# P V of the W2 lanes moved behind them, with ten lent buffers

## The chip, the core and the metric

The kernel runs on one NeuronCore of one Trainium2 chip. The metric is the device time of one execution in microseconds (us). A profile of one execution stands beside the times: it shows each engine's instructions (PE = TensorE matmul, PEld = its weight loads, DVE = VectorE, ACT = ScalarE, POOL = GpSimd, SP = SyncE, which here only issues DMAs), and L12 means line 12 of the kernel.

## What is computed

A transformer block on x of 2048 rows and 576 columns, bf16, with 32 heads of 18 columns, a sliding window of 256 keys, and a gated MLP of width 4608:

```python
def _A_ref(x, wqkv, wo):
    B, S, D = x.shape
    H = 32; Dh = D // H; W = 256
    qkv = (lambda x, *d: x.transpose(*d))((x @ wqkv).reshape(B, S, 3, H, Dh), 2, 0, 3, 1, 4)
    q, k, v = qkv[0], qkv[1], qkv[2]
    scores = jnp.einsum("bhqd,bhkd->bhqk", q, k) * (Dh ** -0.5)
    idx = jnp.arange(S)
    mask = (idx[:, None] - idx[None, :] >= 0) & (idx[:, None] - idx[None, :] < W)
    scores = jnp.where(mask[None, None], scores, -1e9)
    p = _softmax(scores, axis=-1)
    o = jnp.einsum("bhqk,bhkd->bhqd", p, v)
    return (lambda x, *d: x.transpose(*d))(o, 0, 2, 1, 3).reshape(B, S, D) @ wo

def _B_ref(x, w1, w3, w2):
    gate = jnp.einsum("bsd,df->bsf", x, w1)
    up = jnp.einsum("bsd,df->bsf", x, w3)
    h = _silu(gate) * up
    return jnp.einsum("bsf,fd->bsd", h, w2)

x = A_x
xn = _layernorm(x, axis=-1)
return x + _A_ref(xn, A_wqkv, A_wo) + _B_ref(xn, B_w1, B_w3, B_w2)
```

## The kernel before

The rows are worked in four chunks of 512 (c = 0 to 3). The 32 heads are eight groups of four (g = 0 to 7), and two groups make a pair j. Every operation is recorded with `add` (engine, keys read, written and joined), and `resolve` turns the keys into semaphore waits; each engine runs its own operations in the recorded order, SP's DMA queue too. Buffers of the same kind are told apart by keys such as `("w13", 1)`, and a writer waits for the last readers of its key.

A chunk goes through these stages:

- **Gate/up**, 36 units (`unit_pairs`, L860; `unit_tanh`, L869; `unit_h`, L875 and L878). A unit is 9 pairs of 64-row matmuls into one of three pairs of PSUM banks, which `job()` hands out in turn; unit u + 3 takes unit u's banks. The weights come in sets of 512 columns, four units each, in three buffers `w13`; `load_part` (L343) issues the next part, and from chunk 1 on a set has two parts of 576 KB. Between the pairs stand score steps of groups 4 to 7 (`scores` L682, `exps` L691, `masks` L718), and late in the stage their P V (`pv`, L739), two pairs in a row.
- **Projections** of the next chunk's q, k and v (`proj_part`, L496). `pair_of` says which two of nine column tiles one q projection makes; `new_k` and `new_q` copy keys and queries of groups 0 to 3 from `stage` to their places by DMA.
- **W2 lanes** (`w2_lanes`). The array works as four row tiles of 32 rows, one lane each, with W2 (L1036) and the output projection (L1045) in four passes d_ of 128 output columns. A planner with a clock for each lane writes the order: it takes the lane that is least far, and puts in score steps of the next chunk's groups 0 to 3 (`score_new` L756, `exps_new` L763 on ACT, `masks_new` L771 on DVE), 48 of them, at least `W2_SPACE` apart. Two steps share a buffer from `slots`, 14 of them. One round of the lanes is a matmul in each; after round numbers in `events` come repacks of the keys of groups 4 to 7 (`span_main` L585, `span_last` L616; nine, from round 40, 12 apart), the sums of a finished pass sent by a DMA transpose (`turn`, L1119), and at rounds 148 and 156 the two parts of the next chunk's second weight set. `finish` sums a pass's four banks on ACT and DVE (L987 to L992).
- When 24 steps are done and `PV_WAIT` is over, **P V of groups 0 and 1** (`pv_new(n, 0, ...)`, L791, 48 matmuls over all 128 rows and 32-column tiles) stands among the lanes. All lanes stop for it. Its output is emptied by `pv_out` (a transpose on DVE, L800), divided in `o_scale` (L805 on DVE, L806 on POOL) and turned back in `o_turn` (L813); its 12 slots are then used again.
- The **rest of W2**, its last 64 columns (`b = sets[0][0]`, 41 steps of two column tiles, L1086 and L1096), then **P V of groups 2 and 3** (L791), and `orem`/`frem` take the 64 columns out (L1105, L1106).

The next chunk's gate/up then starts with what is left over: x of the old chunk is loaded (`load_four`, L315), the late P V is emptied, and work is put behind unit u by `later(u, ...)`: turns in units 0 and 1, `o_pack` and `o_rest` (L817, DMAs on SP) in units 1 to 5, and the sum with x (`fin_add`, L1130 and L1132; `fin_store`, L1137) in units 4 to 7. Layernorm statistics of the chunk after (`ln_stats`, L391 to L394) start in unit 8 of chunks 1 and 2. The last chunk has no lanes and ends with a stage of its own.

Of the kernel before, what the change touches and what calls it, by code (L numbers as in the profile page):

```python
# [5 lines left out]
dt = mybir.dt  # L6
# [4 lines left out]
_DEBUG = {}  # L11
# [153 lines left out]
def bass_parallel_sum__sliding_block__glu_gated_swiglu__prompt_kernel(  # L165
# [32 lines left out]
    with ExitStack() as es:  # L198
# [39 lines left out]
        def pt_slot(sl):  # L238
            kind, n = sl
            if kind == "pt":  # L240
                return pt[:, n, :, :]
            if kind == "w2":
                return w2[n][:, :, :].rearrange("p f d -> p (f d)")[:, 0:2 * CH].rearrange("p (q r) -> p q r", r=2)
            if kind == "xs":
                return xpb[:, n:n + 2, :].rearrange("p t d -> p (t d)")[:, 0:2 * CH].rearrange("p (q r) -> p q r", r=2)
            if kind == "od":
                return od[n][:, :, :].rearrange("p g c -> p (g c)").rearrange("p (q r) -> p q r", r=2)
            if kind == "sh":
                two = stage[:, 2 * n:2 * n + 2, :]
            else:  # L250
                two = hT[:, NF - 8 + 2 * n:NF - 6 + 2 * n, :]
            return two.rearrange("p t c -> p (t c)").rearrange("p (q r) -> p q r", r=2)

        def pt_keys(sl):
            kind, n = sl
            if kind in ("pt", "w2", "od"):
                return [(kind, n)]
            if kind == "xs":
# [209 lines left out]
        def pair_of(c, i):  # L468

            return (((0, 1), (2, 3), (8, 4), (5, 6)) if c == 0 else ((8, 0), (1, 2), (3, 4), (5, 6)))[i]  # L470

# [486 lines left out]
        def w2_lanes(c, live, pool_):  # L958
# [17 lines left out]
            rounds = 0  # L976
            pv_done = False
# [20 lines left out]
            while any(at[a] < len(items[a]) for a in range(4)):  # L998
# [57 lines left out]
                if a == 3:  # L1056
                    rounds += 1
                    for what in events.pop(rounds, ()):
                        w2_side(c, what)
                if not pv_done and 0 in ended and not any(tail) and min(at) > 2 * 41 + 5 and now > ended[0] + PV_WAIT:  # L1060
                    pv_done = True
                    _DEBUG.setdefault("st", []).append((c, "pv", round(max(clk), 2), d_, at[:]))
                    cand = sorted(sets[1 - d_ % 2], key=lambda x: ready[x])[:2]
                    t = max(clk)
# [11 lines left out]
                    for g in (0, 1):  # L1076
                        for s in range(3):
                            slots.extend(pt_of[(n, g, s, pr)] for pr in range(2))
            assert pv_done and done == len(steps), (c, pv_done, done)
            _DEBUG.setdefault("w2", []).append((c, round(max(clk), 2), ended, [round(x - max(clk), 2) for x in clk]))  # L1080
            b = sets[0][0]
            for k in range(41):
                for r in range(2):
                    if k < NF:
                        sl = (c * 2 * NFC + 16 + k // 18) % NW2
                        add("pe", lambda e, k=k, r=r, sl=sl: e.matmul(  # L1086
                            PS[64 * r:64 * r + 64, b, 0:256], w2_by(sl, 64)[:, k % 18, :], hT[:, k, 256 * r:256 * r + 256],
                            start=(k == 0), stop=False, tile_position=(0, 64 * r), skip_group_check=True),
                            r=[("h", k), ("w2", sl)], **{"j" if k or r else "w": [("ps", b)]})
                        if r and k % 18 == 17:  # L1090
                            load_w2((c + 1) * 2 * NFC)
                    else:
# [4 lines left out]
                            PS[64 * r:64 * r + 64, b, 0:256], wt, oT[:, t, 256 * r:256 * r + 256],  # L1097
                            start=False, stop=(t == 4), tile_position=(0, 64 * r), skip_group_check=True),
# [17 lines left out]
        def w2_side(c, what):  # L1116
            if what[0] == "turn":
                d_ = what[1]
                add("sp", lambda e: e.dma_start_transpose(fin[:, :, d_ * 128:(d_ + 1) * 128], gs[d_ % 2][:]),  # L1119
                    r=[("gs", d_ % 2)], dma=f"tr{d_}", **{"j" if d_ else "w": [("fin", k) for k in range(TB)]})  # L1120
            elif what[0] == "repack":
                k = what[1]
                (span_main if k < 5 else span_last)(GN, G, only=slice(k if k < 5 else k - 5, (k if k < 5 else k - 5) + 1))
            else:
                load_part()

# [165 lines left out]
        W2_FIRST, W2_SPACE, PV_WAIT = 2.2, 0.53, 3.0  # L1292
        W2_REPACK, SEND_AFTER = 40, 15
        W2_EVENTS = {148: (("part",),), 156: (("part",),)}
        late_pv = None

        for c in range(NC):
# [23 lines left out]
            early = [("sh" if c else "h", n) for n in range(4)] + [("w2", (c * 2 * NFC + n) % NW2) for n in range(NW2)]  # L1321
            if c:
                free += [("od", n) for n in range(NOD)]
            side = {}
# [167 lines left out]
            if c + 1 < NC:  # L1492
# [12 lines left out]
                for m, what in enumerate(PROJ_LATER + [None]):  # L1505
# [82 lines left out]
```

## Time and profile before

| what | value |
|---|---|
| three runs, median (lowest to highest) | 554.21 us (553.2 to 554.61) |
| the profiled execution | 553.22 us |
| its span, first to last instruction | 551.5 us |
| lanes between chunks 1 and 2, with the P V inside | 251.3 to 290.6 us |
| 64-column rest of W2 | 290.6 to 295.2 us |
| second P V | 295.2 to 296.6 us |
| first L860 of chunk 2 | 296.6 us |
| granted clock of PE | 1.0 |

In the rows of the timeline the first number is the start, the second the duration, both in us, then engine, line, operation, what is written and read, and how many rows were merged. A matmul's end is modelled and overlaps the next one, so its pace is read from starts. In the groups by line stand the busy time in us, the mean of one in ns, and the idle time before. In the waits stand the total, the number and the longest. "SPq" and "ACTq" are DMA issues; "to landing" is the time from issue until the data have arrived.

### The profile page before, as it was taken

What the parts mean: (1) busy time and instruction counts of PE and PEld (TensorE: products, weight loads), DVE (VectorE), ACT (ScalarE), POOL (GpSimd) and SP (SyncE); (2) the same over time, 40 slices, a digit from 0 to 9 for tenths busy, and PEclk for the clock granted to TensorE, in tenths of its full rate; (3) what the DMA queues carried; (4) which work ended last, traced back from release to release, by engine and by line L of the source; (5) the groups of instructions that cost most, each with busy time, mean ns of one, the idle gap of its engine ahead of it and who ended that gap; (6) DMA issues with size and microseconds to landing.
All of it is one profiled execution on the core that took longest, in us unless ns stands there. A gap on an engine that the chain in (4) does not pass through costs nothing.

```text
span 551.5 us, 17660 instructions
## 1 busy us (share of the span) xinstructions
PE 547.4 (99%) x7690; PEld 302.4 (55%) x7690; DVE 364.5 (66%) x745; ACT 294.5 (53%) x481; POOL 120.5 (22%) x281
## 2 busy tenths in 40 slices
PE   8999999999999999999999999999999999999998
PEld 4555545465564444555556444455555644454776
DVE  6566988746748877874665887786466676688011
ACT  6457776267827565236883655533787376523000
POOL 5613644200013332110001333211000233210000
PEclk9999999999999999999999999999999999999999
DMA  9997999558699999395769999928687988845452
GB/s 232 205 209 147 201 195 187 130 111 165 130 181 196 196 182 172 73 181 119 152 136 201 195 188 183 163 57 172 139 169 140 183 178 170 165 111 137 130 151 64
DMA packets 166070, 88.12 MB, mean 160 GB/s; under 512 B 101546, under 2 KB 163754, under 8 KB 165994
## 3 DMA queue, kind: packets, MB, share of 16 engines
q1 hardware_dynamic: 164622, 85.42, 79.1%
q10 hardware_dynamic: 1372, 1.59, 1.2%
q8 instruction: 60, 0.98, 0.8%
q14 instruction: 16, 0.13, 0.1%
HBM read 71.30 MB, written 2.36 MB: 134 GB/s over the span
## 4 chain that ended last, share of the span: by engine, by line
PE 98%; DMA 1%; SPq 0%; ACT 0%; issue 0%; DVE 0%
PE ps L860 51%; PE ps L1036 17%; PE ps L496 10%; PE ps L932 6%; PE ps L682 4%; PE ps L1086 2%; PE ps L1045 2%; PE ps L739 2%; PE ps L791 2%; PE ps L756 1%; DMA wv<-in_A_wqkv_dram 1%; PE ps L939 1%; PE ps L1096 0%; SPq L311 0%; ACT xnT L447 0%; PE ps L846 0%
## 5 line engine op out<-in xcount | busy, mean ns | idle before, releaser
L860 PE MATMUL ps<-xnT,w 64*128 64x512 bf16 x1400 | 177.0, 376 | 0.0
L860 PE MATMUL ps<-xnS,w 64*128 64x512 bf16 x1120 | 147.8, 376 | 0.0
L875 DVE SCALAR_TENSOR_TENSOR gs<-thb,ps 128x512 bf16<-128x512 bf16 x144 | 97.8, 679 | 60.6 <-ACT thb L869 60.0
L869 ACT ACTIVATE thb<-ps 128x512 bf16<-128x512 f32 x144 | 85.6, 595 | 77.1 <-PE ps L860 76.2
L1036 PE MATMUL ps<-hT,w 32*128 32x512 bf16 x1728 | 106.9, 374 | 0.0
L860 PEld LDWEIGHTS ps<-xnT,w 64*128 64x128 bf16 x1400 | 67.2, 94 | 70.2
L878 DVE SCALAR_TENSOR_TENSOR hT<-gs,ps 128x512 bf16<-128x512 bf16 x144 | 98.9, 687 | 5.0
L860 PEld LDWEIGHTS ps<-xnS,w 64*128 64x128 bf16 x1120 | 53.9, 94 | 58.1
L1036 PEld LDWEIGHTS ps<-hT,w 32*128 32x128 bf16 x1728 | 57.6, 92 | 29.6 <-issue 1.4
L763 ACT ACTIVATE pt<-ps 128x512 bf16<-128x512 f32 x120 | 65.1, 594 | 7.7 <-PE ps L756 7.5
L691 ACT ACTIVATE pt<-ps 128x1024 bf16<-128x1024 f32 (+1 forms) x46 | 46.2, 1005 | 33.5 <-PE ps L682 33.4
L756 PE MATMUL ps<-qv,kn 18*128 18x384 bf16 (+2 forms) x288 | 54.5, 267 | 0.0
L806 POOL TENSOR_TENSOR oq<-uq,rden 128x288 bf16<-128x288 f32 x12 | 8.1, 678 | 194.2 <-DVE rden L805 194.2
L771 DVE TENSOR_TENSOR pt<-pt,kv 128x256 int32<-128x256 int32 x96 | 31.3, 371 | 24.5 <-ACT pt L763 24.1
L718 POOL TENSOR_TENSOR pt<-pt,mk 128x128 int32<-128x128 int32 (+1 forms) x82 | 33.2, 426 | 41.3 <-ACT pt L691 41.3
L496 PE MATMUL ps<-xnT,wp 64*128 64x512 bf16 (+1 forms) x360 | 38.2, 355 | 0.1
L932 PE MATMUL ps<-w,hT 128*128 128x288 bf16 (+1 forms) x292 | 36.9, 284 | 0.0
L756 PEld LDWEIGHTS ps<-qv,kn 18*128 18x128 bf16 x288 | 26.5, 93 | 14.4 <-DVE uq L800 0.8
L932 PEld LDWEIGHTS ps<-w,hT 128*128 128x128 bf16 x292 | 28.2, 98 | 7.4 <-issue 0.5
L682 PE MATMUL ps<-qv,kv 64*128 64x320 bf16 (+4 forms) x336 | 31.7, 258 | 0.0
L813 DVE STREAM_TRANSPOSE od<-oq 128x256 bf16<-128x256 bf16 x64 | 25.4, 425 | 5.5 <-POOL oq L806 5.5
L990 DVE TENSOR_TENSOR thb<-ps,thb 128x512 f32<-128x512 f32 x24 | 16.6, 692 | 18.4 <-ACT thb L987 17.8
(132 smaller groups left out, 529.7 us busy)
## 6 DMA issues: line engine op xcount, KB each, us to landing
w<-in_B_w_dram SPq DMA_DIRECT2D x60, 576.0 KB, 6.9
w<-in_B_w_dram SPq DMA_DIRECT2D x72, 288.0 KB, 3.9
w<-in_B_w_dram SPq DMA_DIRECT2D x12, 192.0 KB, 6.1
xp<-in_A_x_dram SPq DMA_DIRECT2D x4, 576.0 KB, 4.6
xnS<-xnT SPq DMA_DIRECT2D x8, 256.0 KB, 4.8
xp<-in_A_x_dram SPq DMA_DIRECT2D x14, 144.0 KB, 4.0
oT<-od SPq DMA_DIRECT2D x56, 36.0 KB
w<-in_B_w_dram SPq DMA_DIRECT2D x6, 320.0 KB, 5.2
```

The lines of the kernel that those rows point to most:

```text
L496: op = add("pe", lambda e, out_=out_, st=st, mv=mv, n=n, r0=r0, first=first: e.matmul(out_, st, mv, start=first, stop=(part == 1 and n == ...
L682: add("pe", lambda e, r0=r0, out_=out_, kb=kb, q0=q0, nb=nb: e.matmul(out_, kb4[r0:r0 + 64, g - GN, kb + NV - NB, :] if kb < 0 else kv[r0: ...
L691: add("act", lambda e: e.activation(pt_slot(sl)[:, 0:w, :], PS[:, SC[0]:SC[1] + 1, 0:w].rearrange("p r q -> p q r"), ACT.Exp, scale=scale) ...
L718: add("pool", lambda e, vb=vb, mm=mm: e.tensor_tensor(vb, vb, mm, ALU.mult), r=(key if n == 0 else []) + ["mk"], **{"w" if n == 0 else "j" ...
L756: add("pe", lambda e: e.matmul(PS[:, b, c0:c0 + nb * 128], kn[32 * a:32 * a + Dh, g, W + 128 * jb:W + 128 * jb + 128], qv[32 * a:32 * a + ...
L763: add("act", lambda e: e.activation(head_of(sl, p), PS[:, b, :], ACT.Exp, scale=scale), r=[("ps", b)], **{"j" if p else "w": pt_keys(sl)})
L860: op = add("pe", lambda e, n=n, r0=r0, r=r, k=k, src=src: e.matmul(PS[:, b0 + r, :], wt[r0:r0 + 64, k, fl * 128:(fl + 1) * 128], src, star ...
L869: add("act", lambda e: e.activation(th[i][:], PS[:, bg, :], ACT.Tanh, scale=0.5), r=[("ps", bg)], w=[("th", i)])
L875: add("dve", lambda e: e.scalar_tensor_tensor(out=gs[i][:], in0=th[i][:], scalar=1.0, in1=PS[:, bg, :], op0=ALU.add, op1=ALU.mult), r=[("t ...
L878: add("dve", lambda e: e.scalar_tensor_tensor(out=hT[:, u, :], in0=gs[i][:], scalar=0.5, in1=PS[:, bu, :], op0=ALU.mult, op1=ALU.mult), r= ...
L932: add("pe", lambda e: e.matmul(bank, hT[:, f, tt * 128:(tt + 1) * 128], w2[sl][:, k, n0:n1], start=first, stop=(c + 1 == NC and half == 1 ...
L1036: add("pe", lambda e, b=b, rows=rows, wt=wt, fl=fl, k=k, a=a, first=first: e.matmul(PS[:, b, :], wt[rows, fl, :], hT[rows, k, :], start=fi ...
```

## The change

P V of groups 0 and 1 is no longer among the lanes. Both P Vs stand behind the rest of W2, one behind the other, ahead of gate/up. Scoring has 24 slots: new are eight of the nine rows of `w13[1]` ("wt", four), four of the five rows of the old chunk's `xnT` ("xT", two), `od` (two), and one more each from the x and the stage tiles. The two parts of the second weight set wait for the last matmul of the rest of W2 (`load_part((end,))`). The repacks start at round 36 and stand 14 apart. In the rest of W2 the five output-projection steps stand in the middle. `pair_of` is the same for all chunks, and `new_k(0)` and `new_q` come one projection earlier. In the next chunk four banks are emptied instead of two, the turns stand in units 0 to 3, `load_four` in unit 2, `o_pack` and `o_rest` in units 2 to 6, `fin_add` in units 7 to 10, and two `pt` slots serve as `uqs` until unit 3.

```diff
+            if kind == "wt":
+                return w13[1][:, 2 * n:2 * n + 2, :].rearrange("p k f -> p (k f)").rearrange("p (q r) -> p q r", r=2)
+            if kind == "xT":
+                return xnT[:, n // 2, 2 * (n % 2):2 * (n % 2) + 2, :].rearrange("p k f -> p (k f)").rearrange("p (q r) -> p q r", r=2)
...
-            return (((0, 1), (2, 3), (8, 4), (5, 6)) if c == 0 else ((8, 0), (1, 2), (3, 4), (5, 6)))[i]
+            return ((0, 1), (2, 3), (8, 4), (5, 6))[i]
...
-            slots = [("pt", k) for k in range(NPT)] + [("xs", 0), ("xs", 3), ("sh", 0), ("sh", 1)]
+            lent = [(("wt", k), [("w13", 1)]) for k in range(4)] + [(("xT", 2 * (c % 2) + k), xk(c)) for k in range(2)]
+            for sl, keys in lent:
+                P.bufs[sl] = _Gen([], None)
+                P.bufs[sl].readers = [o for k in keys for o in P.bufs[k].writers + P.bufs[k].readers]
+            slots = [("xs", k) for k in (0, 2, 4)] + [sl for sl, _ in lent] + [("pt", k) for k in range(NPT)]
+            slots += [("od", k) for k in range(NOD)] + [("sh", k) for k in range(3)]
...
-            events = {k: list(v) for k, v in W2_EVENTS.items()}
+            events = {}
             for k in range(9):
-                events.setdefault(W2_REPACK + 12 * k, []).append(("repack", k))
+                events.setdefault(W2_REPACK + W2_STEP * k, []).append(("repack", k))
...
-                if not pv_done and 0 in ended and not any(tail) and min(at) > 2 * 41 + 5 and now > ended[0] + PV_WAIT:
-                    pv_done = True
...
-                    pv_new(n, 0, cand)
-                    clk = [t + PV_NEW] * 4
-                    for x in (0, 1):
-                        pv_out(cand[x], x)
-                        ready[cand[x]] = t + PV_NEW + (1.2, 1.9)[x]
-                    o_scale(0)
-                    o_turn(0, 0)
-                    o_turn(0, 1)
-                    o_scale(1)
-                    o_turn(1, 0)
-                    o_turn(1, 1)
...
-            for k in range(41):
+            for k in [*range(18), *range(NF, NF + 5), *range(18, NF)]:
...
-            banks = job()
-            pv_new(n, 1, banks)
+            banks = [job(), job()]
+            end = last_pe()
+            for j in range(2):
+                pv_new(n, j, banks[j])
+            for j in range(2):
+                load_part((end,))
+            for sl, keys in lent:
+                for k in keys:
+                    P.bufs[k].readers += [o for o in P.bufs[sl].readers if o not in P.bufs[k].readers]
...
-        W2_REPACK, SEND_AFTER = 40, 15
-        W2_EVENTS = {148: (("part",),), 156: (("part",),)}
+        W2_REPACK, W2_STEP, SEND_AFTER = 36, 14, 15
...
-                fin_xs[:] = load_four(c - 1)
-                pv_out(late_pv[0], 0)
-                pv_out(late_pv[1], 1)
+                for m in range(2):
+                    sl = free.pop()
+                    uqs[2 + m:] = [pt_slot(sl).rearrange("p q r -> p (q r)").bitcast(dt.float32)]
+                    uq_keys[2 + m:] = [pt_keys(sl)]
+                    later(3, lambda sl=sl: free.append(sl))
+                pv_out(late_pv[0][0], 0)
+                pv_out(late_pv[0][1], 1)
                 o_scale(0)
-                later(0, lambda: (o_turn(2, 0), o_turn(2, 1), o_scale(1)))
-                later(1, lambda: (o_turn(3, 0), o_turn(3, 1)))
-                later(1, lambda: o_pack(0, "sp"))
+                pv_out(late_pv[1][0], 2)
+                pv_out(late_pv[1][1], 3)
+                later(2, lambda c=c: fin_xs.__setitem__(slice(None), load_four(c - 1)))
+                later(0, lambda: (o_turn(0, 0), o_turn(0, 1), o_scale(1)))
+                later(1, lambda: (o_turn(1, 0), o_turn(1, 1), o_scale(2)))
+                later(2, lambda: (o_pack(0, "sp"), o_turn(2, 0), o_turn(2, 1), o_scale(3)))
+                later(3, lambda: (o_turn(3, 0), o_turn(3, 1)))
                 for n in range(7):
-                    later(2 + n // 3, lambda n=n: o_rest(n, "sp"))
-                later(5, lambda: o_pack(1, "sp"))
+                    later(3 + n // 3, lambda n=n: o_rest(n, "sp"))
+                later(6, lambda: o_pack(1, "sp"))
                 for tt in range(TB):
-                    later(4 + tt, lambda tt=tt, c=c: (fin_add(tt), fin_store(c - 1, tt - 1) if tt % 2 else None))
+                    later(7 + tt, lambda tt=tt, c=c: (fin_add(tt), fin_store(c - 1, tt - 1) if tt % 2 else None))
...
-                    if got == ("q", 2):
+                    if got == ("q", 1):
                         new_k(0)
+                    elif got == ("q", 2):
                         new_k(1)
...
-                    if 3 <= m < 7:
-                        new_q(m - 3, "act")
+                    if 2 <= m < 6:
+                        new_q(m - 2, "act")
```

More of the change, by code (lines that the diff above doesn't have):

```diff
@@ L256, in pt_keys @@
             if kind in ("pt", "w2", "od"):
+                return [(kind, n)]
+            if kind in ("wt", "xT"):
                 return [(kind, n)]
@@ L1059, in w2_lanes @@
                         w2_side(c, what)
-                if not pv_done and 0 in ended and not any(tail) and min(at) > 2 * 41 + 5 and now > ended[0] + PV_WAIT:
-                    pv_done = True
-                    _DEBUG.setdefault("st", []).append((c, "pv", round(max(clk), 2), d_, at[:]))
-                    cand = sorted(sets[1 - d_ % 2], key=lambda x: ready[x])[:2]
-                    t = max(clk)
-                    pv_new(n, 0, cand)
-                    clk = [t + PV_NEW] * 4
-                    for x in (0, 1):
-                        pv_out(cand[x], x)
-                        ready[cand[x]] = t + PV_NEW + (1.2, 1.9)[x]
-                    o_scale(0)
-                    o_turn(0, 0)
-                    o_turn(0, 1)
-                    o_scale(1)
-                    o_turn(1, 0)
-                    o_turn(1, 1)
[L1076 to L1079, printed above, removed]
+            assert done == len(steps) and not any(tail), (c, done)
             _DEBUG.setdefault("w2", []).append((c, round(max(clk), 2), ended, [round(x - max(clk), 2) for x in clk]))
             b = sets[0][0]
-            for k in range(41):
+            for k in [*range(18), *range(NF, NF + 5), *range(18, NF)]:
                 for r in range(2):
@@ L1087, in w2_lanes @@
                             PS[64 * r:64 * r + 64, b, 0:256], w2_by(sl, 64)[:, k % 18, :], hT[:, k, 256 * r:256 * r + 256],
-                            start=(k == 0), stop=False, tile_position=(0, 64 * r), skip_group_check=True),
+                            start=(k == 0), stop=(k == NF - 1), tile_position=(0, 64 * r), skip_group_check=True),
                             r=[("h", k), ("w2", sl)], **{"j" if k or r else "w": [("ps", b)]})
@@ L1097, in w2_lanes @@
                             PS[64 * r:64 * r + 64, b, 0:256], wt, oT[:, t, 256 * r:256 * r + 256],
-                            start=False, stop=(t == 4), tile_position=(0, 64 * r), skip_group_check=True),
+                            start=False, stop=False, tile_position=(0, 64 * r), skip_group_check=True),
                             r=key, j=[("ps", b)])
@@ L1120, in w2_side @@
                     r=[("gs", d_ % 2)], dma=f"tr{d_}", **{"j" if d_ else "w": [("fin", k) for k in range(TB)]})
-            elif what[0] == "repack":
+            else:
                 k = what[1]
                 (span_main if k < 5 else span_last)(GN, G, only=slice(k if k < 5 else k - 5, (k if k < 5 else k - 5) + 1))
-            else:
-                load_part()
         def fin_add(tt):
@@ L1321, in bass_parallel_sum__sliding_block__glu_gated_swiglu__prompt_kernel @@
             early = [("sh" if c else "h", n) for n in range(4)] + [("w2", (c * 2 * NFC + n) % NW2) for n in range(NW2)]
-            if c:
-                free += [("od", n) for n in range(NOD)]
             side = {}
```

2 lines of the change are left out of this document (1 added, 1 removed).

## The prediction

> **What bounds the kernel now.** I read the page first (span, busy shares, the chain that ended last), then the waits of PE, then the rows of the stage that the change rewrites.
>
> ```profile
> span 551.5 us, 17660 instructions
> PE 547.4 (99%) x7690; PEld 302.4 (55%) x7690; DVE 364.5 (66%) x745; ACT 294.5 (53%) x481; POOL 120.5 (22%) x281
> ...
> PE 98%; DMA 1%; SPq 0%; ACT 0%; issue 0%; DVE 0%
> ```
>
> ```profile
> PE ps L1160 <- DVE oq L1154: 1.2, 1, 1.2
> PE ps L496 <- DMA wv<-in_A_wqkv_dram: 0.2, 1, 0.2
> ```
>
> PE is the whole chain, and in the whole span it waits 1.4 us, all of it before the first chunk. So no wait can be removed in the parts that change. Time can only come from work that PE does with fewer columns in flight than it could, and it can be lost by any wait that the change brings in. The stage between chunks 1 and 2 stands for all three (the view of windows, columns PE, PEld, DVE, ACT, POOL, clock, DMA share, GB/s):
>
> ```profile
> 251.30:290.60 39.30, 39.30 (x796) 21.82 (x794) 22.62 (x60) 30.14 (x57) 1.35 (x2) 1.00 0.72 139
> 290.60:295.20 4.60, 4.60 (x90) 4.40 (x90) 2.08 (x3) 1.09 (x2) 0.00 (x0) 1.00 1.13 204
> 295.20:296.60 1.40, 1.40 (x51) 1.03 (x50) 0.42 (x1) 0.00 (x0) 0.00 (x0) 1.00 1.18 181
> 296.60:305.00 8.40, 8.40 (x95) 4.10 (x90) 6.01 (x13) 4.54 (x6) 3.60 (x8) 1.00 0.97 204
> ```
>
> Row one is the lanes (L1036, L1045, L756) with the first P V inside, row two the 64-column rest of W2 (L1086, L1096), row three the second P V, row four the first units of gate/up. The granted clock is 1.00 in all of them.
>
> **Part 1, the P V taken out of the lanes.** Its surroundings in the timeline:
>
> ```profile
> 271.21 0.38 PE L1036 MATMUL ps<-hT,w 32*128 32x512 bf16 x4
> ...
> 271.43 0.38 PE L1036 MATMUL ps<-hT,w 32*128 32x512 bf16 x3
> ...
> 271.65 0.38 PE L1036 MATMUL ps<-hT,w 32*128 32x512 bf16 x4
> ...
> 271.96 1.21 PE L791 MATMUL ps<-pt,va 128*20 128x128 bf16 x34
> ...
> 273.38 0.39 PE L1036 MATMUL ps<-hT,w 32*128 32x512 bf16 x2
> ```
>
> The lanes start a round each 0.22 us (271.21, 271.43, 271.65), so the next was due at 271.87. It starts at 273.38. The P V in the lanes therefore costs 273.38 - 271.87 = 1.51 us, of which 0.09 us is the pause before its first matmul (271.96 - 271.87).
>
> **Part 2, the same P V put behind the other's place.** A P V that stands alone ahead of gate/up costs, from its first matmul to the next line's, 296.60 - 295.18 = 1.42 us:
>
> ```profile
> 295.18 0.23 PE L791 MATMUL ps<-stage,va 128*20 128x128 bf16 x2
> ...
> 296.60 0.82 PE L860 MATMUL ps<-xnT,w 64*128 64x512 bf16 x6
> ```
>
> What a second one costs directly behind the first, no row of L791 shows. The older form of P V (L739, chunk 0) shows one alone and two in a row:
>
> ```profile
> 55.31 0.32 PE L739 MATMUL ps<-hT,va 64*20 64x320 bf16 x4
> ...
> 56.30 0.39 PE L682 MATMUL ps<-qv,kv 64*128 64x320 bf16 x4
> ```
>
> ```profile
> 82.03 1.05 PE L739 MATMUL ps<-pt,va 64*20 64x320 bf16 x72
> ...
> 83.95 0.36 PE L682 MATMUL ps<-qv,kv 64*128 64x320 bf16 x4
> ```
>
> One takes 56.30 - 55.31 = 0.99 us, two take 83.95 - 82.03 = 1.92 us, so the second costs 0.93, or 0.06 less than one alone. I carry the 0.06 over: 1.42 - 0.06 = 1.36 us. The bounds are 1.42 (the seam saves nothing) and about 1.28 (nothing but its 3072 columns, at the lanes' pace of 512 in 0.22 us less what each short matmul adds; an estimate). The sum for one stage: 1.51 - 1.36 = 0.15 us won, between 0.09 and 0.23. Three stages: **0.45 us**, between 0.27 and 0.69. A ceiling for what the lanes can give: 162 rounds of 0.216 us and 12 score steps of 512 columns a lane are 37.6 us, with a P V of 1.28 that is 38.9 against 39.3, so 0.4 us a stage, 1.2 us in all, even if every seam vanished.
>
> **Part 3, what covers the rest.** The score steps are the same 48 a stage; ACT is busy 30.14 of 39.30 us (first row above) and will be so in about 37.8 us, 80%. With 24 slots for 24 pairs of steps none waits for a P V any more; each lent buffer (eight of the nine rows of w13[1], four of the five of the old chunk's xnT, od, x and stage tiles) was last read before the lanes or, for stage tiles 4 and 5, by repacks that are issued up to round 92 and are reused by the last pair. Cost zero; uncovered, a late slot would hold ACT and then a lane. The repacks 14 rounds apart end at round 148 of 162 where they ended at 136; their keys are first read in unit 0, over 10 us later (14 rounds, 4.60 and 2.8 us), which hides their landing. The projections' new pair order adds no instruction; new_k's loads on SP and new_q's on ACT go one projection earlier, ahead of the same evacuations.
>
> ```profile
> 238.00:251.30 13.30, 13.30 (x164) 8.25 (x160) 8.07 (x19) 5.57 (x14) 2.04 (x5) 1.00 0.86 162
> ```
>
> In the projections ACT is busy 5.57 of 13.30 us and PE waits for none of its evacuations, so an issue more ahead of one of them is covered; cost zero. The five output-projection matmuls moved inside the 64-column rest change order, not count.
>
> **Part 4, DVE in the first units.** Two pv_outs, two reciprocals and four turns leave the lanes and join the units. The tanh rows give a unit's period, score step included:
>
> ```profile
> 299.68 0.59 ACT L869 ACTIVATE thb<-ps 128x512 bf16<-128x512 f32 x1
> ...
> 301.84 0.59 ACT L869 ACTIVATE thb<-ps 128x512 bf16<-128x512 f32 x1
> ```
>
> It is 301.84 - 299.68 = 2.16 us, and DVE already does this in it:
>
> ```profile
> 301.02 0.69 DVE L878 SCALAR_TENSOR_TENSOR hT<-gs,ps 128x512 bf16<-128x512 bf16 x1
> 301.63 0.76 DVE L813 STREAM_TRANSPOSE od<-oq 128x256 bf16<-128x256 bf16 x2
> 302.32 0.21 DVE L805 RECIPROCAL rden<-ofin 128x16 f32<-128x16 f32 x1
> 302.46 0.69 DVE L875 SCALAR_TENSOR_TENSOR gs<-thb,ps 128x512 bf16<-128x512 bf16 x1
> 303.19 0.69 DVE L878 SCALAR_TENSOR_TENSOR hT<-gs,ps 128x512 bf16<-128x512 bf16 x1
> ```
>
> From hT to hT with a pair of turns and a reciprocal between is 303.19 - 301.02 = 2.17 us: the pattern just fits, and the change runs it in units 0 to 3 where it ran in 0 and 1. The two extra pv_outs come ahead of unit 0's gs, where DVE stands idle until 300.30 (tanh end). Unit 0's hT ends at 301.71 and its banks are next taken by unit 3, at 296.60 + 3 x 2.16 = 303.08: 1.37 us of slack. I cost this at zero and expect at most some 0.5 us of lateness, inside the slack. The smallest margin lies further on: the adds for the output move from units 4 to 7 to units 7 to 10, onto the next chunk's layernorm.
>
> ```profile
> L800 DVE STREAM_TRANSPOSE uq<-ps 128x512 f32<-128x512 f32 x12 | 8.6, 714 | 4.8 <-PE ps L791 2.8 <-PE ps L739 2.0
> ...
> L1130 DVE TENSOR_TENSOR kv<-kv,xp 128x512 bf16<-128x512 bf16 x12 | 5.1, 424 | 0.0
> L1132 DVE TENSOR_TENSOR kv<-kv,xp 128x64 bf16<-128x64 bf16 x12 | 2.7, 226 | 0.0
> ```
>
> ```profile
> 183.25 0.45 DVE L391 BATCH_NORM_STATS2 stats<-xp 128x6 f32<-128x288 bf16 x1
> ...
> 184.89 0.69 DVE L878 SCALAR_TENSOR_TENSOR hT<-gs,ps 128x512 bf16<-128x512 bf16 x1
> ```
>
> ```profile
> 186.66 0.59 PE L860 MATMUL ps<-xnT,w 64*128 64x512 bf16 x4
> ```
>
> In chunk 1 unit 9's hT ends at 184.89 + 0.69 = 185.58 behind the statistics, and unit 12 takes its banks at 186.66: 1.08 us left, from which one pair of adds (0.42 + 0.23 = 0.65 us) is now taken. Some 0.4 us is left, so again zero.
>
> **Part 5, the second weight set.** It is loaded in two parts of 576 KB, near the lanes' end now, behind the last W2 matmul after the change.
>
> ```profile
> L343 SPq DMA_DIRECT2D w<-in_B_w_dram x2: 638/968/1299, 288.1 to 289.4; - x2
> ...
> DMA to landing us min/median/max: 6.5/7.5/8.5
> ```
>
> ```profile
> 293.67 1.25 SPq L1119 DMA_TRANSPOSE kv<-gs  x1
> ```
>
> Let T0 be the first P V's start. On SP the parts stand behind the last turn, which issues from 293.67 to 294.92, just before the P V at 295.18; so they issue at T0 and some 0.65 us later. The pair above landed 289.4 + 8.5 = 297.9, which is 9.8 us after its first issue, behind a W2 piece. Gate/up starts at T0 + 1.36 + 1.42 = T0 + 2.78 and needs the second set in unit 4, 4 x 2.16 us later: T0 + 11.4. Landing at T0 + 9.8 leaves 1.6 us. Cost zero, and this is the thinnest cover that is taken away: before, the set had landed at 297.9 for a use at 305.2. The third set is issued a unit later and stands behind it; the load of four x tiles, which was first in line, now comes in unit 2, and its adds in unit 7. Behind the waiting parts on SP stands only the transpose of the 64-column rest, not read before unit 7.
>
> **The rivals.**
> A (slower): the second set comes late. The trace shows landings up to
>
> ```profile
> L343 SPq DMA_DIRECT2D w<-in_B_w_dram x84: 595/638/1527, 9.1 to 492.5; - x84
> ...
> DMA to landing us min/median/max: 4.4/6.7/11.1
> ```
>
> A second part that took the slowest 11.1 us would land at T0 + 0.65 + 11.1 = T0 + 11.75, 0.35 us late: 1.0 us over three stages, 554.8. If third set and second shared the DMA engines evenly instead of in order, the four parts would need about twice 9.8 less the 4 us of their later issue, T0 + 15.5 or so: 4 us late three times, 566. It decides from T0 + 11.4. Against it: in the row of the pair the first part landed after 6.5 and the second after 8.5, in order; and the parts themselves made most of the DMA share of 1.13 in row two of the windows, so that little is left ahead of them at T0. The Trainium skill's page "DMA: Bandwidth & Descriptors", section "Rules for kernel authors", asks to issue a DMA early and wait late, and the change does the reverse; by that rule this rival's lateness would show. The trace bears it out only as far as the margin shrinks from 7 to 1.6 us.
> B (slower): DVE becomes the bound of the first units. If the extra work there (two pv_outs of 0.7 us, two reciprocals of 0.21, four turns of 0.38, some 3.3 us) found no idle time, it would be 3.3 - 1.37 = 1.9 us late, three times: about 559.5. It decides from 1.37 us of lateness. The 2.17 us rhythm above speaks against it. The Trainium skill's page "TensorEngine Tiling (Array Packing)", section "PSUM Bottleneck", says that tiling speeds PE up and not the emptying of PSUM, which then may bind; by it four emptied banks in a row would give this rival's time. This trace shows room, not the bound.
> C (no change): the change doesn't do what it says for PE: the seam between the two P Vs costs what the lanes' pause did, or the lanes without the P V run into each other elsewhere. Then 0 us, 554.2.
>
> **How the numbers follow.** The profiled execution took 553.22 us with its span of 551.5; less 0.45 it is 552.77. The median of the three runs, 554.21, lies 0.99 above it, and with the same gain it is **553.8**. Chances: forecast 0.78, A 0.10, B 0.05, C 0.07. What a measurement of this kernel can tell from no change is about 0.3%, 1.66 us: faster means under 552.55, slower over 555.87. The forecast with its ceiling (1.2 us, 553.0) and the spread of the runs (1.0 below the median, 0.4 above) reaches past 552.55 in 0.05; A and B pass 555.87 in 0.07 and 0.04. So faster 0.05, same 0.84, slower 0.11. The range: 553.0 less 0.6 of spread, 552.4, up to A's 554.8 and 0.8 of spread, 555.6.
>
> **What would show it.** Right: the lanes last about 37.8 us, the two P Vs about 2.8 us, the first unit follows without a wait, PE's waits still list only the two rows above. Wrong: a wait of L860 for a DMA of w (A), of L860 for DVE hT or uq (B), or a stretch of the lanes and P Vs together as long as the 39.3 + 1.4 us of before (C). A gain over 1.2 us would mean that the lanes held a loss that I haven't seen.

## The result and the profile after

Six runs of the changed kernel took 559.35 us in the median (557.56 to 561.36), six of the kernel before on the same chip 553.9 (553.2 to 555.11). The ratio is 1.0097, with a 95% interval of 1.007 to 1.0124: the change costs about 5.4 us, or 1%. The forecast was 553.8 us, with a range up to 555.6. The profiled execution took 558.82 us, 5.6 more than that of before.

The page of the kernel after shows a span 5.6 us longer, the same work on PE, and a chain in which PE is no longer alone:

```profile
span 557.1 us, 17660 instructions
PE 547.4 (98%) x7690; PEld 305.7 (55%) x7690; DVE 365.8 (66%) x745; ACT 294.5 (53%) x481; POOL 119.9 (22%) x281
...
PE 95%; DMA 2%; SPq 1%; issue 1%; DVE 0%; ACT 0%
```

Its waits of PE (total, number, longest) have a new first row, a wait of the gate/up matmul (L860 before, L866 now). Four smaller rows, 2.0 us in all, lie ahead of chunk 1 and aren't shown:

```profile
PE ps L866 <- issue: 4.1, 3, 1.8
PE ps L1156 <- DVE oq L1150: 1.2, 1, 1.2
```

"issue" means that the view names no releaser; the releaser has to be found from the times, below. The windows of the stages that the change touches, first the lanes between chunks 1 and 2, the rest of W2 and the P Vs, then gate/up of chunks 1 and 2 (columns as in the prediction):

```profile
255.65:293.38 37.73, 37.73 (x746) 20.11 (x745) 20.14 (x52) 30.19 (x57) 0.00 (x0) 1.00 0.70 142
293.38:297.98 4.60, 4.60 (x87) 4.40 (x84) 2.08 (x3) 1.08 (x2) 0.00 (x0) 1.00 0.07 16
297.98:300.71 2.73, 2.73 (x99) 2.08 (x98) 1.67 (x4) 0.00 (x0) 0.00 (x0) 1.00 0.46 111
162.02:242.55 80.53, 77.40 (x945) 39.68 (x940) 63.80 (x124) 39.74 (x55) 23.33 (x55) 1.00 0.96 170
300.71:379.44 78.73, 77.65 (x945) 39.96 (x940) 63.48 (x122) 39.84 (x55) 22.83 (x54) 1.00 0.93 169
```

The same two gate/up stages of the kernel before:

```profile
161.14:238.19 77.05, 77.05 (x946) 37.47 (x940) 61.92 (x117) 39.74 (x55) 22.17 (x53) 1.00 0.89 166
296.60:373.66 77.06, 77.06 (x945) 37.48 (x940) 61.81 (x115) 39.86 (x55) 21.68 (x52) 1.00 0.86 162
```

The stage that was rewritten became shorter: 37.73 + 4.60 + 2.73 = 45.06 us, where before it was 39.30 + 4.60 + 1.40 = 45.30. The loss is in the stage behind it. Chunk 1's gate/up takes 80.53 - 77.05 = 3.48 us longer, chunk 2's 78.73 - 77.06 = 1.67, chunk 3's nothing. Less twice the 0.24 us of the stages between, that is 4.7 of the 5.6 us. The other 0.9 lie ahead of chunk 1's gate/up (162.02 against 161.14). Chunk 0's gate/up stands there, whose code the change doesn't touch; it has two waits of 0.79 and 0.39 us in this execution, and it took between 79.8 and 82.8 us in the profiled executions of this study. So the 0.9 us say nothing of the change.

**Which wait.** PE's timeline of the kernel after, at the first and the longest of the three waits (the third, 0.99 us, is chunk 2's); the idle time ahead of a row stands in brackets:

```profile
195.52 0.38 PE L866 MATMUL ps<-xnT,w 64*128 64x512 bf16 x2
197.24 1.04 PE L866 MATMUL ps<-xnT,w 64*128 64x512 bf16 x8 [1.34 <-issue]
...
205.45 0.40 PE L866 MATMUL ps<-xnT,w 64*128 64x512 bf16 x2
207.63 1.04 PE L866 MATMUL ps<-xnT,w 64*128 64x512 bf16 x8 [1.79 <-issue]
```

The first wait lies ahead of unit 16, which is the first unit of the fifth weight set, the second ahead of unit 20, the first of the sixth. By the starts of the units they account for all of chunk 1's loss: unit 15 starts 31.78 us behind the stage's first matmul before and after, unit 16 1.50 us later than before, and unit 20 another 1.97 us. In chunk 2, 1.15 of the 1.67 us come at unit 16. The rows of the two parts of the fifth set (issued 188.9 and 189.6), and of the sixth (195.3 and 196.0), give their landing:

```profile
L349 SPq DMA_DIRECT2D w<-in_B_w_dram x2: 657/672/688, 188.9 to 189.6; - x2
...
DMA to landing us min/median/max: 5.4/6.5/7.5
```

```profile
L349 SPq DMA_DIRECT2D w<-in_B_w_dram x2: 622/753/884, 195.3 to 196.0; - x2
...
DMA to landing us min/median/max: 8.4/10.0/11.6
```

189.6 + 7.5 = 197.1 and PE goes on at 197.24; 196.0 + 11.6 = 207.6 and PE goes on at 207.63. The weights are late, and because SP issues them late: the fifth set is issued 26.9 us behind the stage's first matmul (188.87 - 162.02), before it was 20.5 (181.62 - 161.14), and it then takes 7.5 us at most, no more than the 8.9 of before.

**Why SP issues late.** SP's timeline, kernel after, from unit 4 (oT<-od are `o_pack` and `o_rest`, oT<-oT is the last `o_rest`, which reads what the first four wrote):

```profile
171.69 1.84 SPq L823 DMA_DIRECT2D oT<-od  x3
173.57 1.35 SPq L349 DMA_DIRECT2D w<-in_B_w_dram  x2
174.96 2.11 SPq L823 DMA_DIRECT2D oT<-od  x3
185.21 0.54 SPq L823 DMA_DIRECT2D oT<-oT  x1
185.79 3.04 SPq L823 DMA_DIRECT2D oT<-od  x4
188.87 1.39 SPq L349 DMA_DIRECT2D w<-in_B_w_dram  x2
```

The same stretch of the kernel before:

```profile
171.02 1.28 SPq L817 DMA_DIRECT2D oT<-od  x2
172.34 2.06 SPq L343 DMA_DIRECT2D w<-in_B_w_dram  x2
174.66 0.53 SPq L817 DMA_DIRECT2D oT<-oT  x1
175.24 3.12 SPq L817 DMA_DIRECT2D oT<-od  x4
178.40 3.17 SPq L1137 DMA_DIRECT2D out_dram<-kv  x2
181.62 1.40 SPq L343 DMA_DIRECT2D w<-in_B_w_dram  x2
```

Before, the copies `o_rest(0)` to `o_rest(5)` were issued ahead of the fourth set's two parts (172.34), and the dependent copy came 0.26 us behind those parts. After, one unit later, `o_rest(3)` to `o_rest(5)` stand behind the parts (174.96 against 173.57). The dependent copy waits for the landing of `o_rest(3)`, the first of these three, and SP with it. The rows of the three copies, of which the view has one landing, and of the two parts ahead of them:

```profile
L823 SPq DMA_DIRECT2D oT<-od x3: 598/699/731, 175.0 to 176.5; - x3
...
DMA to landing us min/median/max: 10.2/10.2/10.2
```

```profile
L349 SPq DMA_DIRECT2D w<-in_B_w_dram x2: 638/651/664, 173.6 to 174.3; - x2
...
DMA to landing us min/median/max: 8.9/9.8/10.7
```

The second part lands at 174.3 + 10.7 = 185.0, the small copy behind it at 175.0 + 10.2 = 185.2, and at 185.21 SP goes on. A copy of 16 KB took 10.2 us with 1.15 MB of weights just ahead of it; before, such copies stood ahead of those parts and took 4.1 to 5.0. SP stood from 174.96 + 2.11 = 177.07 to 185.21, 8.1 us. Behind it were the four issues of `o_pack(1)`, 3 us, and behind these the fifth set. The sixth is late behind the fifth: two stores, a transpose and a load of x stand between them (190.30 to 195.25).

The Trainium skill's page "DMA: Bandwidth & Descriptors", section "Queues, rings and completion order", says that each DMA engine consumes the descriptors of a ring in their order, but that DMAs of one issuing engine need not complete first in, first out. The landing of the small copy 0.2 us behind the large one agrees with the first; no row here bears on the second.

### The profile page after: what moved, and what is told of

The parts are those of the page before. It is cut to its first block, busy times and chain, and to the rows that moved or that the text cites. A ratio compares the mean times of both kernels' runs of the same rounds, so it can differ in the third digit from the quotient of the medians.

```text
span 557.1 us, 17660 instructions
## 1 busy us (share of the span) xinstructions
PE 547.4 (98%) x7690; PEld 305.7 (55%) x7690; DVE 365.8 (66%) x745; ACT 294.5 (53%) x481; POOL 119.9 (22%) x281
## 4 chain that ended last, share of the span: by engine, by line
PE 95%; DMA 2%; SPq 1%; issue 1%; DVE 0%; ACT 0%
PE ps L866 48%; PE ps L1046 16%; PE ps L502 10%; PE ps L938 6%; PE ps L688 3%; PE ps L1077 2%; PE ps L745 2%; PE ps L1055 2%; PE ps L762 2%; DMA kv<-stage 1%; PE ps L797 1%; SPq L591 1%; PE ps L945 1%; DMA xp<-in_A_x_dram 0%; PE ps L1087 0%
## 5 line engine op out<-in xcount | busy, mean ns | idle before, releaser
L866 PE MATMUL ps<-xnT,w 64*128 64x512 bf16 x1400 | 178.5, 376 | 4.2 <-issue 4.1
L866 PE MATMUL ps<-xnS,w 64*128 64x512 bf16 x1120 | 148.7, 376 | 0.0
L866 PEld LDWEIGHTS ps<-xnT,w 64*128 64x128 bf16 x1400 | 70.1, 94 | 72.3 <-issue 6.1
L866 PEld LDWEIGHTS ps<-xnS,w 64*128 64x128 bf16 x1120 | 56.5, 94 | 55.8 <-issue 0.4
L697 ACT ACTIVATE pt<-ps 128x1024 bf16<-128x1024 f32 (+1 forms) x46 | 46.2, 1005 | 37.8 <-PE ps L688 37.8
L812 POOL TENSOR_TENSOR oq<-uq,rden 128x288 bf16<-128x288 f32 x9 | 6.1, 677 | 196.8 <-DVE rden L811 196.8
L762 PEld LDWEIGHTS ps<-qv,kn 18*128 18x128 bf16 x288 | 26.9, 93 | 19.3
L769 ACT ACTIVATE pt<-ps 128x512 bf16<-128x512 f32 x60 | 32.7, 594 | 0.7 <-PE ps L762 0.7
L697 ACT ACTIVATE stage<-ps 128x1024 bf16<-128x1024 f32 x12 | 12.3, 1023 | 30.8 <-PE ps L688 30.8
L688 PEld LDWEIGHTS ps<-qv,kv 64*128 64x128 bf16 x336 | 16.9, 94 | 18.4 <-DMA kv<-stage 1.3
## 6 DMA issues: line engine op xcount, KB each, us to landing
xp<-in_A_x_dram SPq DMA_DIRECT2D x4, 576.0 KB, 10.7
```

The lines of the kernel that those rows point to most:

```text
L688: add("pe", lambda e, r0=r0, out_=out_, kb=kb, q0=q0, nb=nb: e.matmul(out_, kb4[r0:r0 + 64, g - GN, kb + NV - NB, :] if kb < 0 else kv[r0: ...
L697: add("act", lambda e: e.activation(pt_slot(sl)[:, 0:w, :], PS[:, SC[0]:SC[1] + 1, 0:w].rearrange("p r q -> p q r"), ACT.Exp, scale=scale) ...
L762: add("pe", lambda e: e.matmul(PS[:, b, c0:c0 + nb * 128], kn[32 * a:32 * a + Dh, g, W + 128 * jb:W + 128 * jb + 128], qv[32 * a:32 * a + ...
L769: add("act", lambda e: e.activation(head_of(sl, p), PS[:, b, :], ACT.Exp, scale=scale), r=[("ps", b)], **{"j" if p else "w": pt_keys(sl)})
L866: op = add("pe", lambda e, n=n, r0=r0, r=r, k=k, src=src: e.matmul(PS[:, b0 + r, :], wt[r0:r0 + 64, k, fl * 128:(fl + 1) * 128], src, star ...
```

## The experiments

Three theories were to be told apart. **Q**: the order on SP's queue, as just told; `o_rest` a unit later puts the copies behind the fourth set, SP stands, the fifth set is late. **D**: the data; the second weight set and x of the old chunk, which moved into the start of gate/up, fill the DMA engines there, so that all that follows lands late. **V**: DVE; its extra work and the sums on top of the layernorm delay it, and with it what waits for it. Every experiment is the changed kernel with the edit shown, but e4, which is the kernel before. Each has 11 or 12 runs, e6 has 6; the ratio is to the kernel before on the same chip.

Of V the changed kernel's own trace says much already: in chunks 1 and 2 every unit up to 15 starts as far behind the first matmul as before, so nothing that DVE does late reaches PE ahead of unit 16.

**e1: `o_rest` back in its unit, all else changed.**

```diff
-                    later(3 + n // 3, lambda n=n: o_rest(n, "sp"))
+                    later(2 + n // 3, lambda n=n: o_rest(n, "sp"))
```

> The changed kernel with o_rest put back into units 2 to 4 (it stands in 3 to 5 in the change), so that its copies stand ahead of the third weight set's successor in SP's queue. Theory Q (SP's queue is held by the copy oT<-oT, which waits for copies that stand behind weight parts): that wait falls from 22.5 us in three to under 6, the fifth set is issued some 7 us earlier, L866's waits in chunks 1 and 2 are gone, and the time is 553.3 to 554.5. Theory D (the second weight set and the x tiles, moved into gate/up, are more than DMA can carry there): the parts land as late as in the changed kernel, 558.5 to 560. Theory V (DVE is late with the adds on the layernorm): no change, 558.5 to 560.

Measured: 552.91 us (552.08 to 554.12), ratio 0.9985, interval 0.9972 to 0.9999. All of the loss is gone, by one number in one line. SP's timeline:

```profile
171.91 3.80 SPq L823 DMA_DIRECT2D oT<-od  x6
175.75 1.40 SPq L349 DMA_DIRECT2D w<-in_B_w_dram  x2
182.10 0.53 SPq L823 DMA_DIRECT2D oT<-oT  x1
182.68 3.14 SPq L823 DMA_DIRECT2D oT<-od  x4
185.86 1.38 SPq L349 DMA_DIRECT2D w<-in_B_w_dram  x2
```

The copies are all ahead of the parts again, and no matmul of L866 waits. But two of Q's figures are missed: SP still stands 175.75 + 1.40 to 182.10, 4.9 us, and 13.9 us in the three chunks where under 6 was expected (22.5 in the changed kernel, 2.2 before), and the fifth set is issued 23.6 us behind the first matmul, 3.3 us earlier than in the changed kernel and not 7. The copies now take 6.9 to 8.3 us to land, with the second set and x moved ahead of them. So D is at work too, and here it is covered.

**e2: the second weight set back in the lanes, `o_rest` late.**

```diff
-            events = {}
+            events = {148: [("part",)], 156: [("part",)]}
...
-            for j in range(2):
-                load_part((end,))
...
+            elif what[0] == "part":
+                load_part()
```

> The changed kernel with the two parts of the second weight set back at rounds 148 and 156 of the lanes. Theory Q alone: the copy oT<-oT still waits for copies behind weight parts, some 5 us instead of 7.5 since less stands ahead of them; the fifth set comes some 5 us late and most of the loss stays, 556.5 to 559. Theory D: the backlog is gone and with it the loss, 553.3 to 554.5, and the wait of oT<-oT falls to 1 or 2 us. Theory V: no change, 558.5 to 560.

Measured: 556.99 us (554.09 to 558.99), ratio 1.0053, interval 1.0037 to 1.007. About half of the loss is left (3.0 of 5.4 us), as Q expects, but the trace puts it down in part to another wait. With less data ahead, SP stands 6.2 us at the longest where it stood 8.1, and the fifth set is issued at 188.06. L866's waits in the trace are 2.2 us, and 1.12 of them lie in unit 0, where the fifth set has no part; that wait comes again in e5. Nor is all of the data back: x is still loaded in unit 2, ahead of the copies.

**e3: only the dependent copy moved, behind the fifth set (unit 9).**

```diff
-                    later(3 + n // 3, lambda n=n: o_rest(n, "sp"))
+                    later(9 if n == 6 else 3 + n // 3, lambda n=n: o_rest(n, "sp"))
```

> The changed kernel with nothing but the copy oT<-oT (o_rest 6) moved from unit 5 to unit 9, behind the fifth set's parts. The bytes that DMA carries stay as in the changed kernel. Theory Q: SP isn't held any more, the fifth set is issued by unit 8 as in the kernel before, L866 doesn't wait, 553.3 to 554.8. Theory D: the same bytes in the same stage, so most of the loss stays, 557.5 to 560. Theory V: no change, 558.5 to 560.

Measured: 553.64 us (552.33 to 554.73), ratio 0.9991, interval 0.9978 to 1.0003. Here all the data move as in the changed kernel and the other six copies stand where it has them. Only the instruction that holds SP comes later, and the fifth set is issued at 179.42, 18.3 us behind the first matmul:

```profile
174.14 5.24 SPq L823 DMA_DIRECT2D oT<-od  x7
179.42 1.86 SPq L349 DMA_DIRECT2D w<-in_B_w_dram  x2
```

D alone would have left the loss. It takes the held queue.

**e4: the kernel before, with `o_rest` a unit later.**

```diff
-                    later(2 + n // 3, lambda n=n: o_rest(n, "sp"))
+                    later(3 + n // 3, lambda n=n: o_rest(n, "sp"))
```

> The kernel before with o_rest one unit later (units 3 to 5), as in the change, and nothing else of it. Theory Q in its plain form (the order alone costs): the fifth set is issued late here too, 556 to 559. Q and D together (the copies have to stand behind the parts, and DMA has to be behind by the second set): the wait of oT<-oT grows to some 5 us, but the parts ahead of it land 4 us earlier than in the changed kernel, so that the fifth set comes 3 us late against 4 us of slack: 553.5 to 555. Theory V: 553.9, no change.

Measured: 554.34 us (553.27 to 557.08), ratio 1.001, interval 0.9995 to 1.0025. Q in its plain form falls here: the order alone does not cost 5 us in the median. It does bring the mechanism to the edge: SP stands 7.8 us at the longest, the fifth set is issued at 187.58, and in the profiled execution, one of the longer ones (555.54 us), the same wait is there:

```profile
PE ps L860 <- issue: 2.1, 2, 1.9
```

Together with e1 this says that it takes both, the order (Q) and the data ahead (D).

**e5: the P V in a row alone.** `o_rest`, the second set, the load of x and the sums all back in their places; e1's and e2's edits, and

```diff
+                fin_xs[:] = load_four(c - 1)
...
-                later(2, lambda c=c: fin_xs.__setitem__(slice(None), load_four(c - 1)))
...
-                    later(7 + tt, lambda tt=tt, c=c: (fin_add(tt), fin_store(c - 1, tt - 1) if tt % 2 else None))
+                    later(4 + tt, lambda tt=tt, c=c: (fin_add(tt), fin_store(c - 1, tt - 1) if tt % 2 else None))
```

> The row of P Vs with the buffers alone: o_rest in units 2 to 4, the second set's parts in the lanes, the x tiles loaded first and the adds in units 4 to 7, all as in the kernel before. Theory Q: no hold of SP beyond 2 us a stage and no wait of L866, and the row's gain of 0.2 us a stage stands alone: 552.8 to 553.6. Theory D (bytes in gate/up still cost in the version with o_rest early): 0.5 us or more faster than that version, 552.4. Theory V: no lateness of DVE on the layernorm, the same as Q.

Measured: 554.1 us (552.32 to 555.49), ratio 1.0003, interval 0.9989 to 1.0016. A miss: 0.5 us above the expected. SP hardly stands now, but PE waits in unit 0 of chunk 1:

```profile
161.70 0.39 PE L866 MATMUL ps<-xnT,w 64*128 64x512 bf16 x2
163.16 0.82 PE L866 MATMUL ps<-xnT,w 64*128 64x512 bf16 x6 [1.07 <-issue]
```

No releaser is named and no weight is due there: unit 0 reads the first set. e2 shows the same (162.62, 1.12 us), and both have the second set in the lanes; the kernel before has it there too and doesn't show the wait. The DMA records of these two traces hold a lead. The queue q8, kind "instruction", moves blocks of 16 KB, one for some 256 instructions of PE (60 blocks, 15,380 instructions). The block ahead of the wait came 425 and 449 instructions after the one before it, and it ended at 161.75 in e5 and 162.36 in e2, 1.4 us before PE went on in both (163.16, 163.75). So PE may have run out of instructions behind the full DMA queues. No run tests this.

**e6: load of x first and sums in units 4 to 7, `o_rest` late.** e5's last edit alone. It gives DVE back its order of before, so that V would see the loss go.

> The changed kernel with the x tiles loaded ahead of unit 0 and the adds back in units 4 to 7; o_rest stays late and the second set stays behind W2. Theory V (DVE's lateness on the layernorm is what costs): gs starts on time in units 9 to 13 and the loss is gone, 553 to 554.5. Theory Q: DVE is on time and the loss stays, since oT<-oT still holds SP some 7.5 us a stage; with the two stores now ahead of the fifth set's parts on SP rather 1 us more a stage than less, 558.5 to 562.

Measured: 565.92 us (564.28 to 570.52), ratio 1.0234, interval 1.0195 to 1.0272: the loss is not gone, it is more than doubled, and greater than either theory had said. Waits of PE and of SP's queue:

```profile
PE ps L866 <- issue: 9.3, 3, 3.3
...
SPq L823 <- DMA oT<-od: 25.6, 3, 9.1
```

V falls: DVE is on time (unit 11's hT ends 1.2 us ahead of unit 14, in the changed kernel 0.07) and PE waits more. The stores of the sums (out_dram) now stand in the held queue ahead of the fifth set, which is issued at 190.26. Here the view of that set's two parts names who waited for it:

```profile
L349 SPq DMA_DIRECT2D w<-in_B_w_dram x2: 673/680/688, 190.3 to 191.0; - x2
...
  PEld ps L866: 3.8, 1
  PE ps L866: 3.3, 1
...
DMA to landing us min/median/max: 6.0/6.9/7.9
```

The three waits, 9.3 us, are not all. Behind two of them PE ran at half its clock, behind the third it didn't (windows, columns as above):

```profile
199.00:202.00 3.00, 3.00 (x20) 1.37 (x22) 0.00 (x0) 0.67 (x1) 0.00 (x0) 0.50 1.15 222
339.00:342.00 3.00, 3.00 (x16) 1.19 (x14) 0.00 (x0) 0.00 (x0) 0.00 (x0) 0.50 1.13 213
```

The waits ahead were 3.33 and 2.92 us long, the third, with the clock at 1.00 behind it, 3.10. By the starts of units 16 and 17 this cost another 1.5 us each time. In the changed kernel, then, the later load of x and the later sums, whose place on DVE the prediction had called the narrowest, together saved some 6.6 us (565.92 - 559.35), of which some 3 are this clock.

**e7: the dependent copy behind `o_pack(1)` (unit 7).** As e3, with 7 in place of 9.

> The changed kernel with oT<-oT in unit 7, behind o_pack(1) but still ahead of the fifth set's parts. Theory Q: SP is held to the same moment, some 24 us after the first L866, but the four copies of o_pack (3 us of issues) are already out, so that the fifth set's parts are issued 3 us earlier than in the changed kernel, as in the version with o_rest early: no wait of L866 in chunks 1 and 2 or one under 0.3 us, 553.2 to 554.5. Theory D: nothing is taken from DMA, 557.5 to 560.

Measured: 553.49 us (552.63 to 556.81), ratio 1.0001, interval 0.9987 to 1.0016. The four issues of `o_pack(1)` no longer stand behind the wait, yet SP stands 6.0 us at the longest, and the fifth set goes out 24.8 us behind the first matmul, 2.1 us earlier than in the changed kernel where 3 was expected: just early enough in most executions. The profiled one was its slowest (556.81 us); unit 16 of chunk 1 doesn't wait in it, but unit 20 and two units of chunk 2 do, 1.2 us in all, where none or under 0.3 was expected.

**e8: e1 and e3 together.**

```diff
-                    later(3 + n // 3, lambda n=n: o_rest(n, "sp"))
+                    later(9 if n == 6 else 2 + n // 3, lambda n=n: o_rest(n, "sp"))
```

> The changed kernel with o_rest in units 2 to 4 and the copy oT<-oT alone in unit 9: both remedies at once. Theory Q: nothing is left to win over either, 552.7 to 553.7, with SP's wait for oT<-od under 3 us in three. Theory D: 552.7 to 553.7 as well if the version with o_rest early has no loss left.

Measured: 553.66 us (552.39 to 554.41), ratio 0.9986, interval 0.9976 to 0.9997. It is e1's result once more, with the fifth set out at 180.46 and no wait of SP for oT<-od.

The profiled executions side by side. In an undisturbed chunk 1 unit 16 starts 33.7 us behind the stage's first L866, so then the fifth set is due. The columns are, for the fifth set, first issue and last landing after that first matmul, what the landing is late by, then PE's wait ahead of unit 16 in the trace, and the median of all runs.

| kernel | issue | landing | late by | PE's wait | median us |
|---|---|---|---|---|---|
| e8 | 18.1 | 31.7 | - | 0 | 553.66 |
| e3 | 18.3 | 31.0 | - | 0 | 553.64 |
| before | 20.5 | 30.1 | - | 0 | 553.9 |
| e5 | 21.8 | 31.6 | - | 0 | 554.1 |
| e1 | 23.6 | 32.0 | - | 0 | 552.91 |
| e7 | 24.8 | not in the trace | | 0 | 553.49 |
| e2 | 25.8 | 34.5 | 0.8 | 0 (unit 0's wait came first) | 556.99 |
| e4 | 26.6 | 35.7 | 2.0 | 1.92 | 554.34 (this one 555.54) |
| after | 26.9 | 35.1 | 1.4 | 1.34 | 559.35 |
| e6 | 28.5 | 37.1 | 3.4 | 3.33 | 565.92 |

In these executions an issue up to about 25 us behind the first matmul loses nothing at unit 16; behind that a microsecond of lateness is a microsecond of PE. e4's profiled execution lies above its median, so it shows the edge and not the usual run, and what makes the changed kernel so much dearer than e4 in the median is shown only in part: its sixth set is late as well (1.79 us), and so is chunk 2's fifth (0.99 us, in e4 0.18). Two of its six runs, not profiled, list a mean clock of 0.997; a slow stretch as in e6 would do that, which isn't shown.

## Why the prediction was wrong

**Parts 1 and 2 held.** Lanes 37.73 us (about 37.8 said), two P Vs 2.73 (2.78 said). The stage gains 45.30 - 45.06 = 0.24 us in these windows, where 0.15 was said, between 0.09 and 0.23: the mechanism as forecast, the size at the upper bound. Taking the P V out gave the lanes 39.30 - 37.73 = 1.57 us (1.51 said), and as the second of two it cost 2.73 - 1.40 = 1.33 (1.36 said). Its lower bound of 1.28 has no row: 3072 columns at 512 in 0.22 us are 1.32. From the last gate/up matmul of a chunk to the first of the next the three stages are 0.24, 0.25 and 0.23 us shorter, 0.7 in all, in the trace of the changed kernel as in those of e1 and e8. Without the loss, e1 and e8 have ratios of 0.9985 and 0.9986, or some 0.8 us, which fits; but the intervals reach 0.9999 and 0.9997, and e3 and e7, without the loss in the median too, can't be told from no change.

**Part 3 held for what it costed.** PE's waits list no score step of the lanes and, behind chunk 0, no matmul of the projections.

**Part 4 held, with less to spare than said.** In unit 9 "some 0.4 us" was to be left. The narrowest place came in unit 11 of chunk 1, behind the layernorm:

```profile
190.16 0.68 DVE L881 SCALAR_TENSOR_TENSOR gs<-thb,ps 128x512 bf16<-128x512 bf16 x1
190.87 0.69 DVE L884 SCALAR_TENSOR_TENSOR hT<-gs,ps 128x512 bf16<-128x512 bf16 x1
```

hT ends at 191.56, and unit 14 takes its banks at 191.63, so 0.07 us were left. It held, and rival B did not occur.

**Part 5 held for the second set and failed behind it.** The second set landed at 160.1 + 8.8 = 168.9:

```profile
L349 SPq DMA_DIRECT2D w<-in_B_w_dram x2: 653/680/707, 159.4 to 160.1; - x2
...
DMA to landing us min/median/max: 5.5/7.2/8.8
```

Unit 4 needed it at 170.7, a margin of 1.8 us where 1.6 was said. (The third set, said to be issued a unit later, goes out 3.2 us behind the first matmul in both kernels.) The step that failed is the next sentence: "Behind the waiting parts on SP stands only the transpose of the 64-column rest". It looked at one place of SP's queue, the parts at T0. The same diff moved `o_pack` and `o_rest` a unit later, past the parts that are issued in unit 4, and this move, named in the text on the change, had no price in any part: neither its issues, nor the wait that one of its copies holds on SP, nor what stands behind that wait. The rows for it were in the trace of before: the dependent copy there came 0.26 us behind two parts of 576 KB, and hardly waited, with all that it waits for ahead of them. The parts land up to 8.9 us after issue in that stretch of before, and a copy put behind them can take as long. In its place the runs showed SP held for 8.1 us, the fifth set issued 6.4 us later in its stage, and 3.5 us lost in chunk 1 and 1.7 in chunk 2.

Rival A had the right kind of mechanism, a weight set that comes late, and priced it at 554.8 to 566. But it named the second set, for the reason that its own transfer might be slow, and the set that was late was the fifth. The second set was on time and still took part: its 1.15 MB now stand ahead of the copies. e1 (the data moved, the order kept: no loss) and e4 (the order moved, the data kept: 0.4 us) show that neither does it alone.

## What to carry to other kernels

When an issue is moved, walk its whole queue: which waits come to stand in front of which transfers, and what is issued behind them. A small copy that a later issue on the same queue waits for belongs ahead of the large transfers, or the instruction that waits belongs behind the next urgent one; either of the two edits takes the whole loss back here, and with the copies in their old place (e1) the change is at best a trace faster than before, at a ratio of 0.9985, too little to call it faster. And a margin that has been used up unseen is a cost that waits for the next edit: e7 has the fifth set out 4.3 us later than before at no cost in the median, and 2 us more, in the changed kernel, go with a loss of 1%.

## What the runs showed of the hardware

A DMA of 16 KB took 10.2 us to land behind two of 576 KB on the same queue; ahead of them it took up to 8.3 us with the second set and x moved in front (e1), and 4.1 to 5.0 in the kernel before. The issue that waited for it, itself 0.54 us long, held its queue for 8.1 us. After waits of 3.33 and 2.92 us PE's granted clock read 0.50 for the next three microseconds (e6); after waits of 3.10 us (e6) and of 1.34 and 1.79 us (the changed kernel) it read 1.00. And a wait of 1.1 us in the first unit of gate/up, seen in two kernels (e2, e5) with no releaser in the profile, ended 1.4 us after a block of PE's instructions had arrived; that the block was the cause isn't shown.
